# Keeping the emitted order of the matmuls in both feed-forward networks, from chunk 3 on

## The chip, the cores and the metric

The kernel runs on one core of one Trainium2 chip. A core has TensorE (PE in the profile, its weight loads PEld), VectorE (DVE), ScalarE (ACT), GpSimd (POOL), SyncE (SP, which here only issues transfers) and 16 DMA engines. The metric is the device time of one execution in microseconds (us); lower is better.

## The reference

One input x of 2048 tokens by 512 channels goes through two branches, and a gate for each token mixes their results:

```python
g = sigmoid((x * gate_w).sum(-1))
a = attention(x, wqkv) @ wo          # 32 heads of 16; each token looks at 8 keys, 2 tokens apart
b = (gelu(x @ w_gate) * (x @ w_up)) @ w_down      # 512 -> 1792 -> 512
out = g * a + (1 - g) * b
```

Everything is float32.

## The kernel before

The tokens are split into two parities of 1024 tokens (`par` 0 and 1). Since the attention's keys lie an even number of tokens apart, each parity is an attention problem of its own. The whole runs in one stream: the projections of parity 0, the feed-forward network (FFN) of parity 0 with `ffn(0)`, the projections of parity 1, `ffn(1)`, and the output projection. The attention of eight units (two parities by four groups of heads) is vector work on DVE; the generator `attention` hands it out piece by piece, and `pull` places pieces of it among the matmuls. The first DVE operation of a piece is `paced` (L357): it waits until the matmul that was emitted last before it has run.

Each FFN goes over 14 chunks `f` of 128 hidden channels. In a chunk, `gate_up` (L557) computes gate and up for two halves of 512 tokens by seven block products instead of eight; the operands a11, a12, a22 come from x itself (tiles A), and s1 to s4 are sums of blocks of x (tiles S); b11, b21, b22 and t1 to t4 are the weights and their sums (tiles g). Every operand is split into a high and a low part, so that `product` (L490) issues six matmuls: two blocks of 128 channels, and for each high by high, high by low and low by high. Each matmul streams 512 columns. The result of a product stands in a PSUM bank "p", of which there are four.

Around the products stand, in this order of emission: a11 (bank X, copied by ACT into bank W at L575), s1 (bank Z), the product a22 of the chunk before (`fourth`, L520, runs the closure `last` of L603), s2 (X), a12 (W, then gelu on ACT, L590), s4 (Z, then `add`, L505, on DVE), and s3 (X, then `add`). `hidden` (L508) makes the hidden values of a half: a multiplication on DVE (L509), the high part on ACT (L511, tile hh) and the low part on DVE (L512, tile hl). The first half is finished in its own chunk, after s4; the second half after a22, which is emitted in the next chunk.

The down projection takes the chunks by pairs `gr`. `down` (L527) handles 128 tokens: six matmuls, three for each chunk of the pair (hh by the high weights, hh by the low weights, hl by the high weights; tiles hh, hl and d), into one of the four banks "acc" for the first token half (b = 0), and into a bank "p" for the second (b = 1), where ACT copies the sum so far in (L532) and out again (L554). From chunk 2 on, each chunk emits four such pieces: chunk f handles the pair f // 2 - 1, so an even chunk f is the first to use the hidden values and weights of chunk f - 1. I call the four pieces of a chunk D0 and D1 (first half) and D2 and D3 (second half). The last pair follows after chunk 13, as eight pieces in a row.

The weights are prepared a chunk ahead: `fetch` and `fetch_d` load them (SP), `combine` (L430) forms the sums t1 to t4 on DVE, `operands` (L439) writes the negated low part on ACT and adds the raw weights with an accumulating DMA that POOL issues (L453, tiles g), and `down_w` (L478) does the same for the down weights (L481 on ACT, L482 on POOL, tiles d). L481 is paced behind s1.

What is emitted is not what runs in this order. The program is built with `schedule_with_timeline_sim=True`: a scheduler plays it through on a simulated timeline and lays down, for each engine, the order in which the instructions are ready there, with the emitted order as priority. `ordered` (L360) adds a dependency without a semaphore: it only tells the scheduler that an instruction stands behind another on the same engine. `LAST` holds the matmul that was emitted last.

```python
def ordered(ins, other):
    after(ins, other, mybir.DependencyClass.NoSync)
...
                if gr == 1 and b == t == 0 and not par:
                    ordered(ins, LAST[-1])
```

Before the change only the six matmuls of one piece (pair 1, first tile, parity 0) are ordered so.

Of the kernel before, what the change touches and what calls it, by code (L numbers as in the profile page):

```python
# [47 lines left out]
def tile_gated_mix(ctx: ExitStack, tc: tile.TileContext, xt, wqkv, wff, wo, out):  # L48
    nc = tc.nc
# [10 lines left out]
    def tl(tag, dt=F32):  # L60
        return pool.tile([P, COLS.get(tag, 512)], dt, name=tag, bufs=BUFS[tag])
# [5 lines left out]
    def bank(tag):  # L67
        return psum.tile([P, 512], F32, name=tag, bufs=BUFS.get(tag, 1))
# [5 lines left out]
    LAST = []  # L74
    idle = [bank("p") for _ in range(4)]
    for i in range(WARM):
        c = i // 4 % 2 * QW
        LAST[:] = [nc.tensor.matmul(idle[i % 4][:, c:c + QW], warm[:, :P], warm, start=not c, stop=True,
                                    skip_group_check=True)]
# [171 lines left out]
    def project_one(par, jj):  # L251

        ps = bank(f"acc{jj % BT}")
        qkv_mm(ps, par, jj, 2, range(KC))
        take(ps, par, jj, 1, False, tag=None if jj < 5 else "c")
        pull(2.2)
        if jj == NP - 1:
            done.add((par, 2))
# [93 lines left out]
    def after(ins, other, cls=mybir.DependencyClass.Sync):  # L352

        tc.add_manual_dep(ins.ins, other.ins.name, mybir.DependencyInfo(cls, mybir.DependencyReason.SCHED_ONLY),
                          reason="pace")
# [4 lines left out]
    def ordered(ins, other):  # L360
        after(ins, other, mybir.DependencyClass.NoSync)
# [39 lines left out]
    def pull(budget, key=None):  # L401
        credit[0] += budget
        while credit[0] > 0 and (key is None or key not in done):
            with tc.high_priority(offset=-BEHIND):
                c = next(fill, None)
            if c is None:
                credit[0] = 0.0
                return
            credit[0] -= c
        if key:  # L410
            credit[0] = 0.0
# [27 lines left out]
    def operands(par, f, i):  # L439


        n = len(GROUPS[i]) * QW
        w = tl(f"g{i}", F32R)
        hi, lo = w[:, :n], w[:, n:2 * n]
        for k, op in enumerate(GROUPS[i]):
            WG[f, op] = hi[:, k * QW:(k + 1) * QW], lo[:, k * QW:(k + 1) * QW]
        if par and not i:
            nc.sync.dma_start(w[:, :2 * n].bitcast(F32), WS[f, i])
            yield
            return  # L450
        raw = RAW[f][:, (0, 4)[i] * QW:][:, :n]
        nc.scalar.activation(lo, raw, AF.Copy, scale=-1.0)  # L452
        nc.gpsimd.dma_start(lo.bitcast(F32), raw, accum_op=OP.add)  # L453
        if not i:
            KEEP[f] = w[:, :2 * n]
        yield
        ins = nc.scalar.activation(hi, raw, AF.Copy)  # L457
        if f:
            paced(ins)
# [30 lines left out]
    def product(ps, a, w, start):  # L490
        for kc in range(2):
            ah, al = XOP[a, kc]
            wh, wl = (x[:, kc * P:(kc + 1) * P] for x in w)
            for n, (w_, a_) in enumerate(((wh, ah), (wh, al), (wl, ah))):
                LAST[:] = [nc.tensor.matmul(ps, w_, a_, start=(start and kc == 0 and n == 0),  # L495
                                            stop=(kc == 1 and n == 2), skip_group_check=True)]

    def copy(ps):
        s = tl("s")
# [12 lines left out]
        nc.vector.tensor_tensor(hl_, ge, hh_.bitcast(F32), op=OP.subtract)  # L512
        Hs[key] = hh_, hl_

    late, COPIED = [], []

    def pace(par, f):
        return PACE[2 if par else f > 5]

    def fourth():  # L520
        if late:
            late.pop()()
# [4 lines left out]
    def down(par, gr, t, b):  # L527
        if b == t == gr == 0:
            ACC.update((t, bank(f"acc{t}")) for t in range(BT))
        pp = bank("p") if b else ACC[t]  # L530
        if b and gr:
            nc.scalar.activation(pp, RT[BT + t], AF.Copy)  # L532
        ts = slice(t * P, (t + 1) * P)
        for i in range(2):
            hh_, hl_ = Hs[2 * gr + i, b]
            d = WD[2 * gr + i]
            for n, (a, w) in enumerate(((hh_, d[:, :512]), (hh_, d[:, 512:1024]), (hl_, d[:, :512]))):
                ins = nc.tensor.matmul(pp, a[:, ts], w, start=(i == 0 and n == 0 and gr == 0),  # L538
                                       stop=(i == 1 and n == 2), skip_group_check=True)
                if gr == 1 and b == t == 0 and not par:  # L540
                    ordered(ins, LAST[-1])
                LAST[:] = [ins]
        jj = BT * b + t
        if gr == NG - 1 and par:
            nc.scalar.activation(pp, pp, AF.Copy, scale=gc[:, par, jj:jj + 1])
            ACC[jj] = pp
        elif gr == NG - 1:
            st = tl("s")
            nc.scalar.activation(st, pp, AF.Copy, scale=gc[:, par, jj:jj + 1])
            nc.gpsimd.dma_start(out_v[2 * jj], st)  # L550
        elif b:
            if gr == 0:
                RT[BT + t] = tl("rt")
            nc.scalar.activation(RT[BT + t], pp, AF.Copy)  # L554
        pull(1.2 * pace(par, 2 * gr + 2))
# [87 lines left out]
    def ffn(par):  # L643
        XOP.update(((n, kc), X[par, blk, kc + k]) for n, blk, k in (("a11", 0, 0), ("a12", 0, 2), ("a22", 1, 2))
                   for kc in range(2))
        todo = iter(())
        for f in range(FC):
            do = {}

            def at(i, x, *args):  # L650
                do.setdefault(i, []).append(lambda: x(*args))

            if f > 1:
                pieces = [[lambda b=b, i=i: down(par, f // 2 - 1, f % 2 * 2 + i, b)] for b in range(2) for i in range(2)]
            else:
                tile_ = (lambda jj: project_one(1, jj)) if par else values
                pieces = [[lambda jj=jj: tile_(jj) for jj in jjs]
                          for jjs in (((0, 1), (2, 3), (4, 5), ()),
                                      ((6,), (7,), (), ()) if par else ((6, 7), (), (), ()))[f]]
            if f + 1 < FC:  # L660
                for i in range(2):
                    steps = operands(par, f + 1, i)
                    at(1 + 2 * i - (not par and f == 1), next, steps, None)
                    at(5 + i - (not par and f == 1), next, steps, None)
                at(0 if f != 1 else 5, fetch_d, f + 1)
                if f == 1 and not par:
                    for g_ in range(2):
                        at(3, down_split, g_)
                for g_ in ((), (0, 1) if par else ())[f] if f < 2 else (f,):
                    steps = down_w(g_)  # L670
                    at(2 if f > 2 else 4, next, steps, None)
                    at(7, next, steps, None)
            else:
                steps = down_w(f)
                at(1, next, steps, None)
                at(4, next, steps, None)
            if par:
                if f + 2 < FC:
                    at(0, fetch_sums, f + 2)
                else:  # L680
                    at(0, fetch_o) if f + 2 == FC else None
                if f + 1 == FC:
                    todo = chain(load_o(), channels_of(0, 0))
                    for i in range(1, 9):
                        at(i, next, todo, None)
            else:
                if f + 2 < FC:
                    at(1, fetch, f + 2)
                    at((4, 5, 6)[f] if f < 3 else 8, combine, f + 2)
                else:  # L690
                    at(0, fetch_x, 1, f + 2 - FC)
                if f + 1 < FC:
                    do.setdefault(0, []).insert(0, lambda: keep(f + 1))
                at(0, keep_parts, f)
                if f + 2 == FC:
                    at(8, early)
                if f + 1 == FC:
                    todo = before()
                    for i in range(2, 9):
                        at(i, next, todo, None)  # L700
            gate_up(par, f, pieces, do)
        for _ in todo:
            pass
        fourth()
        if par:
            out_first()
            oT = {}
        for b in range(2):
            for t in range(BT):
                down(par, NG - 1, t, b)  # L710
                if par and t == 0:
                    oT[0, b] = channels(par, 0, b)
                if not par and not b:
                    split_kq() if t % 2 else again(0, 1 + t)
                elif not par and b:
                    again(1, (2, 3, 0, 1)[t])
        if par:
            finish(oT)
# [452 lines left out]
```

## Time and profile before

| what | value |
|---|---|
| median of three runs | 608.14 us (606.92 to 609.78) |
| the profiled execution | 609.76 us |
| span of its profile, first to last instruction | 608.0 us |
| PE busy | 598.2 us, 2802 matmuls |
| DVE busy | 526.5 us |
| ACT busy | 382.9 us |
| POOL busy | 79.1 us |
| mean granted TensorE clock | 0.999 |

The profiled execution lasts 1.76 us longer than its span, and it stands near the upper end of the three runs. PE is the engine whose waits count. Its busy time is that of pipelined instructions: a matmul is shown with 0.39 us while the next begins after 0.23 us, so a wait shows as a gap in the starts rather than as idle time of the same length. In the rows below, L495 is a product, L538 a piece of the down projection, and the letters after the arrow are the operands.

### The profile page before, as it was taken

Reading aid. Unit: us, or ns where it says so; the run is one execution under the profiler, and the core shown is the slowest. Engines: PE = TensorE matmul, PEld = TensorE weight load, DVE = VectorE, ACT = ScalarE, POOL = GpSimd, SP = SyncE. Lnnn points to the kernel's source line nnn. Section 1 sums busy time; section 2 is a strip of 40 time slices with the busy share of each in tenths; the row PEclk is TensorE's granted clock in tenths of the full one; section 3 lists DMA queues with packets and bytes.
Section 4 is the critical chain, followed back from the end, with each engine's and each line's share of the span. In section 5 each row is a group of like instructions: output and inputs, shape, how many; then the busy total and the mean of one; then the engine's idle time right before and its main releaser. Section 6 shows DMA issues by size and latency. Waiting matters only on the chain.

```text
span 608.0 us, 8192 instructions
## 1 busy us (share of the span) xinstructions
PE 598.2 (98%) x2802; PEld 498.2 (82%) x2802; DVE 526.5 (87%) x611; ACT 382.9 (63%) x650; POOL 79.1 (13%) x106
## 2 busy tenths in 40 slices
PE   9999999999999999989999999999999999999997
PEld 6889977788888887877899888888888888888885
DVE  5997969999898998798989988789899999999941
ACT  5845557777679776857364356566866676677531
POOL 0501001111111111102000001111101111101200
PEclk9999999999999999999999999999999999999999
DMA  7289896989889888976789979686888768937823
GB/s 279 85 252 246 241 275 172 271 237 271 206 248 260 223 255 230 253 205 181 253 218 335 252 221 271 146 256 158 228 207 213 207 182 217 259 88 207 125 50 138
DMA packets 84741, 131.03 MB, mean 216 GB/s; under 512 B 8030, under 2 KB 52317, under 8 KB 84700
## 3 DMA queue, kind: packets, MB, share of 16 engines
q1 hardware_dynamic: 63310, 94.01, 47.7%
q0 software_dynamic: 12096, 31.40, 27.3%
q10 hardware_dynamic: 9294, 5.11, 2.8%
q8 instruction: 22, 0.36, 0.2%
q14 instruction: 19, 0.16, 0.1%
HBM read 67.18 MB, written 36.77 MB: 171 GB/s over the span
## 4 chain that ended last, share of the span: by engine, by line
PE 71%; DMA 12%; issue 8%; DVE 4%; ACT 3%; SPq 1%; ACTq 0%; POOL 0%; POOLq 0%; DVEq 0%
PE p L495 29%; PE p L538 9%; PE acc L189 9%; PE acc L538 9%; PE p L767 5%; DMA d<-r 4%; DMA g<-raw 3%; PE p L834 3%; PE acc L834 3%; DMA ws<-g 3%; DVE prod L290 2%; PE p L189 2%; PE acc L767 2%; DMA kq<-qs 1%; DMA vs<-hl 1%
## 5 line engine op out<-in xcount | busy, mean ns | idle before, releaser
L495 PE MATMUL p<-S,g 128*128 128x512 f32 x672 | 166.5, 390 | 0.0
L495 PEld LDWEIGHTS p<-S,g 128*128 128x128 f32 x672 | 125.7, 188 | 26.5 <-ACT rt L554 0.5
L495 PE MATMUL p<-A,g 128*128 128x512 f32 x504 | 127.6, 390 | 0.1
L495 PEld LDWEIGHTS p<-A,g 128*128 128x128 f32 x504 | 94.3, 188 | 20.4 <-DMA g<-raw 0.6
L290 DVE TENSOR_TENSOR prod<-kq 128x2048 f32<-128x2048 f32 x32 | 73.0, 2281 | 12.3 <-DMA kq<-qs 4.6
L453 POOL DMA_DIRECT2D g<-raw x40 | 34.8, 870 | 319.0 <-ACT g L452 180.5
L331 DVE TENSOR_TENSOR prod<-v,lg 128x2048 f32<-128x2048 f32 x32 | 72.9, 2277 | 1.8 <-PE acc L538 1.3
L293 DVE TENSOR_REDUCE lg<-prod 128x128 f32<-128x2048 f32 x32 | 73.0, 2282 | 0.3
L538 PE MATMUL p<-d,hh 128*128 128x512 f32 x224 | 68.0, 390 | 1.0 <-ACT p L532 0.5
L538 PE MATMUL acc<-d,hh 128*128 128x512 f32 x224 | 61.3, 392 | 3.3 <-DMA d<-r 2.9
L538 PEld LDWEIGHTS acc<-d,hh 128*128 128x128 f32 x224 | 41.8, 188 | 13.5 <-DMA d<-r 3.8
L538 PEld LDWEIGHTS p<-d,hh 128*128 128x128 f32 x224 | 41.9, 188 | 10.5 <-ACT p L532 0.9
L457 ACT ACTIVATE g<-raw 128x1024 fp32r<-128x1024 f32 (+1 forms) x40 | 39.5, 990 | 13.3 <-PE p L495 13.3
L509 DVE TENSOR_TENSOR c<-c 128x512 f32<-128x512 f32 x56 | 38.2, 683 | 9.2 <-ACT c L606 8.8
L505 DVE TENSOR_TENSOR c<-p,s 128x512 f32<-128x512 f32 x56 | 37.9, 682 | 8.1 <-PE p L495 8.1
L500 ACT ACTIVATE s<-p 128x512 f32<-128x512 f32 x56 | 33.2, 592 | 18.1 <-PE p L495 16.5
L452 ACT ACTIVATE g<-raw 128x1024 fp32r<-128x1024 f32 (+1 forms) x40 | 39.5, 986 | 7.9 <-DVE raw L434 6.9
L538 PE MATMUL p<-d,hl 128*128 128x512 f32 x112 | 42.3, 390 | 0.0
L512 DVE TENSOR_TENSOR hl<-c,hh 128x512 fp32r<-128x512 f32 x56 | 38.3, 685 | 4.5 <-ACT hh L511 4.2
L511 ACT ACTIVATE hh<-c 128x512 fp32r<-128x512 f32 x56 | 35.1, 626 | 7.4 <-DVE c L509 6.5
L554 ACT ACTIVATE rt<-p 128x512 f32<-128x512 f32 x48 | 28.1, 592 | 18.1 <-PE p L538 17.8
L335 DVE TENSOR_TENSOR prod<-prod 128x1024 f32<-128x1024 f32 x32 | 39.0, 1219 | 0.3
(193 smaller groups left out, 916.2 us busy)
## 6 DMA issues: line engine op xcount, KB each, us to landing
g<-raw POOLq DMA_DIRECT2D x27, 512.0 KB, 6.1
raw<-wff SPq DMA_DIRECT2D x42, 256.0 KB, 3.4
ws<-g SPq DMA_DIRECT2D x14, 768.0 KB, 5.6
g<-ws SPq DMA_DIRECT2D x14, 768.0 KB, 5.1
r<-wff SPq DMA_DIRECT2D x28, 256.0 KB, 3.7
d<-r POOLq DMA_DIRECT2D x26, 256.0 KB, 7.2
g<-raw POOLq DMA_DIRECT2D x13, 384.0 KB, 7.5
v<-vs SPq DMA_DIRECT2D x8, 512.0 KB, 7.3
```

The costliest lines, as they stand in the source:

```text
L189: LAST[:] = [nc.tensor.matmul(ps[:, :cn], a[:, t], w[:, c0:c0 + cn], start=(kc == 0 and n == 0), stop=(kc == KC - 1 and n == 2))]
L290: paced(nc.vector.tensor_tensor(prod, spans(k, jj), q[:, jj:jj + 2, None, :].to_broadcast([P, 2, W, UC]), op=OP.mult))
L293: nc.vector.tensor_reduce(two_of(lg, jj), prod.rearrange("p j w (h d) -> p (j w) h d", d=DH), axis=AX.X, op=OP.add)
L331: paced(nc.vector.tensor_tensor(prod.rearrange("p j w (h d) -> p (j w) h d", d=DH), spans(v, jj).rearrange("p j w (h d) -> p j w h d", d=D ...
L335: nc.vector.tensor_tensor(prod[:, :, :4], prod[:, :, :4], prod[:, :, 4:], op=OP.add)
L452: nc.scalar.activation(lo, raw, AF.Copy, scale=-1.0)
L457: ins = nc.scalar.activation(hi, raw, AF.Copy)
L495: LAST[:] = [nc.tensor.matmul(ps, w_, a_, start=(start and kc == 0 and n == 0), stop=(kc == 1 and n == 2), skip_group_check=True)]
L509: nc.vector.tensor_tensor(ge, ge, up, op=OP.mult)
L512: nc.vector.tensor_tensor(hl_, ge, hh_.bitcast(F32), op=OP.subtract)
L538: ins = nc.tensor.matmul(pp, a[:, ts], w, start=(i == 0 and n == 0 and gr == 0), stop=(i == 1 and n == 2), skip_group_check=True)
L767: ins = nc.tensor.matmul(pa, a, b, start=(first and n == 0), stop=(last and n == 2), skip_group_check=True)
```

## The change

From chunk 3 on in both FFNs, each matmul of a product and of a down piece is ordered behind the matmul emitted before it. In parity 0 this also covers all pieces of the pairs from 1 on, the eight closing ones among them; the eight closing pieces of parity 1 are not covered. No instruction is added or taken away, and no semaphore wait is asked for; the scheduler gets a fixed order for PE in these stretches, and orders the other engines against it anew.

```diff
@@ product
-                LAST[:] = [nc.tensor.matmul(ps, w_, a_, start=(start and kc == 0 and n == 0),
-                                            stop=(kc == 1 and n == 2), skip_group_check=True)]
+                ins = nc.tensor.matmul(ps, w_, a_, start=(start and kc == 0 and n == 0), stop=(kc == 1 and n == 2),
+                                       skip_group_check=True)
+                if KEPT:
+                    ordered(ins, LAST[-1])
+                LAST[:] = [ins]
...
-    late, COPIED = [], []
+    late, COPIED, KEPT = [], [], []
@@ down
-                if gr == 1 and b == t == 0 and not par:
+                if gr and not par or KEPT:
                     ordered(ins, LAST[-1])
                 LAST[:] = [ins]
@@ ffn
         for f in range(FC):
             do = {}
+            KEPT[:] = [f] if f > 2 else []
...
         fourth()
+        KEPT.clear()
         if par:
             out_first()
```

## The prediction, made before the result was known

> **What bounds the kernel now.** I read the page first, then PE's windows by chunk, PE's waits, and the timeline of single chunks.
>
> ```profile
> span 608.0 us, 8192 instructions
> ...
> PE 598.2 (98%) x2802; PEld 498.2 (82%) x2802; DVE 526.5 (87%) x611; ACT 382.9 (63%) x650; POOL 79.1 (13%) x106
> ...
> PEclk9999999999999999999999999999999999999999
> ```
>
> PE is busy 98% of the span, at full clock in every slice. How much room is left in the stretches that the change touches is told by the pace of the matmuls. The chain of waits has a run without a gap, and the windows give the chunks (us, PE busy and count; the last three columns are clock, DMA share, GB/s):
>
> ```profile
> 576.90 5.44 PE p L538 x24
> ```
>
> ```profile
> 104.18:150.33 46.15, 46.12 (x201) 1.00 0.95 255
> ...
> 165.29:180.68 15.39, 15.26 (x68) 1.00 0.87 240
> ...
> 210.60:225.56 14.96, 14.96 (x68) 1.00 0.86 247
> 225.56:242.09 16.53, 15.27 (x68) 1.00 0.98 246
> ...
> 257.05:284.32 27.27, 25.09 (x109) 1.00 0.66 195
> ```
>
> 24 matmuls in 5.44 us are 0.2267 us each: a group of six takes 1.36 us, a chunk of eleven groups (seven products, four down pieces) 14.96 us. The chunk at 210.60 takes just that and waits for nothing. The one at 165.29 loses 15.39 - 14.96 = 0.43 us, the one at 225.56 loses 1.57 us, and the close of the first FFN, 18 groups or 24.48 us, loses 2.79 us (the 109th record begins before the window). The sum, **4.8 us or 0.8%**, is all that an order can win in the first FFN; chunks 3 to 5, up to 150.33, are busy 46.12 of 46.15 us. In the second it can win nothing; PE is busy throughout (PE, PEld, DVE, ACT, POOL):
>
> ```profile
> 391.78:551.06 159.28, 159.28 (x704) 132.00 (x703) 147.89 (x154) 107.15 (x174) 18.36 (x22) 1.00 0.76 204
> ```
>
> [...]
>
> Who caused the 4.8 us is in PE's waits (total, times, longest) and in the timeline:
>
> ```profile
> PE acc L538 <- DMA d<-r: 2.9, 2, 1.7
> PE p L538 <- ACT p L532: 0.5, 1, 0.5
> ...
> PEld acc L538 <- DMA d<-r: 3.8, 2, 2.1
> ...
> PEld p L495 <- DMA g<-raw: 0.6, 1, 0.6
> ```
>
> ```profile
> 210.60 2.88 PE L495 MATMUL p<-A,g 128*128 128x512 f32 x12
> 213.32 1.97 PE L538 MATMUL acc<-d,hh 128*128 128x512 f32 x8
> ...
> 216.04 2.88 PE L495 MATMUL p<-S,g 128*128 128x512 f32 x12
> ...
> 221.48 2.88 PE L495 MATMUL p<-S,g 128*128 128x512 f32 x12
> ...
> 225.56 2.88 PE L495 MATMUL p<-A,g 128*128 128x512 f32 x12
> 228.28 0.39 PE L538 MATMUL acc<-d,hh 128*128 128x512 f32 x1
> 229.93 1.89 PE L538 MATMUL acc<-d,hh 128*128 128x512 f32 x7 [1.26 <-DMA d<-r]
> ...
> 260.49 1.89 PE L538 MATMUL acc<-d,hh 128*128 128x512 f32 x7 [1.68 <-DMA d<-r]
> ...
> 275.35 0.73 PE L538 MATMUL p<-d,hh 128*128 128x512 f32 x2 [0.50 <-ACT p L532]
> ```
>
> The reader is to see an order that is not the emitted one. A chunk runs a11 and the old a22 (A, x12), then twelve matmuls on "acc", then s1 and s2, a12, D2, s4 and s3, D3. Eight high-part matmuls in a row on "acc" cannot be D0 and D1 as emitted, whose low parts stand between. Counting groups back from 284.32 us, where the FFN ends, the "acc" work at 228.28 (chunk 11) and 258.41 (chunk 13) is the half of the next pair that needs only the even chunk just finished. So the scheduler pulls it a chunk ahead, onto down weights whose accumulating transfer has not landed.
>
> **The change part by part.** It adds no instruction, DMA or semaphore; nothing moves past the queues of SP or POOL except by what the scheduler orders anew. The order becomes a11, D0, s1, old a22, s2, D1, a12, s4, D2, s3, D3.
>
> *What goes.* The pulled-ahead use goes: an even chunk's weights are first used two chunks later. I count the chunk's 1.57 and the row's 1.68 us. The wait for ACT's copy into a bank "p" (0.50) sits in the closing pieces; four pieces on "acc" now stand ahead of those on "p" and cover it. Together 3.75, **3.8 us**. The 0.43 us at 165.29 stay: a11's third matmul waits for the weights' transfer, and a11 keeps its place.
>
> *Odd chunks' down weights* are still used one chunk on. Their rows in chunk 10, their transfers in the chain, and the median on the page:
>
> ```profile
> 218.09 0.62 ACT L481 ACTIVATE d<-r 128x512 fp32r<-128x512 f32 x1
> ```
>
> ```profile
> 219.00 10.88 DMA d<-r
> ...
> 249.64 10.80 DMA d<-r
> ```
>
> ```profile
> d<-r POOLq DMA_DIRECT2D x26, 256.0 KB, 7.2
> ```
>
> L481 is paced behind s1, which now ends 4.08 us into the chunk and not 6.80. At best the issue moves from 8.40 (219.00 - 210.60) to 5.7 us, and the slow 10.88 us land at 16.6. D0 of the next chunk needs them in its fifth matmul, at 14.96 + 1.36 + 0.91 = 17.2: in time. If POOL keeps its order (L482 behind two transfers of L453), landing is at 8.4 + 10.9 = 19.3, 2.1 us late; with the median, 15.6, in time. So from 0 to two slow transfers at 2.1 = 4.2 us; I take 0, by the median row.
>
> *The hidden values are what is late next.* For an even chunk the emitted order gives each half one distance. First half: from the end of s4 come D2, s3, D3, a11 and five matmuls until D0 reads hl: 4 x 1.36 + 1.13 = **6.57 us**. Second half: from the end of a22 come s2, D1, a12, s4 and five matmuls to D2's hl, again 6.57. Between lie add or gelu, multiplication, hh and hl, with attention pieces of about 2.3 us queued on DVE in between. Four readings, first half in chunk 11 of the second FFN and chunk 10 of the first, second half of chunks 7 and 9:
>
> ```profile
> 517.36 0.62 PE L538 MATMUL p<-d,hh 128*128 128x512 f32 x2
> ...
> 518.77 0.68 DVE L505 TENSOR_TENSOR c<-p,s 128x512 f32<-128x512 f32 x1
> 519.37 2.27 DVE L293 TENSOR_REDUCE lg<-prod 128x128 f32<-128x2048 f32 x1
> ...
> 521.56 0.68 DVE L505 TENSOR_TENSOR c<-p,s 128x512 f32<-128x512 f32 x1
> ...
> 524.96 0.68 DVE L512 TENSOR_TENSOR hl<-c,hh 128x512 fp32r<-128x512 f32 x1
> ```
>
> ```profile
> 226.97 0.69 DVE L512 TENSOR_TENSOR hl<-c,hh 128x512 fp32r<-128x512 f32 x1
> ```
>
> ```profile
> 183.40 1.52 PE L495 MATMUL p<-S,g 128*128 128x512 f32 x6
> ...
> 184.78 1.28 ACT L606 ACT_TABLE_LOAD   x1
> ...
> 190.97 0.68 DVE L512 TENSOR_TENSOR hl<-c,hh 128x512 fp32r<-128x512 f32 x1
> ```
>
> ```profile
> 216.44 0.68 DVE L512 TENSOR_TENSOR hl<-c,hh 128x512 fp32r<-128x512 f32 x1
> ```
>
> s4 ended at 517.36 and hl at 525.64: 8.28 us, **1.71 late** by the new distance. In chunk 10 s4 ended at 222.84 (half of the x12 at 221.48) and hl at 227.66: 4.82, in time. a22 ended at 183.40 and hl at 191.65, a table load between: 8.25, 1.68 late. a22 ended at 213.32 and hl at 217.12: 3.80. Before, PE ran other groups meanwhile; now it must stand still.
>
> Such first uses are 22: five even chunks (4 to 12) and the ordered close in the first FFN, five in the second, two halves each. The ends are 0 and half of them at 1.7, 18.7 us. In the new order D2 stands between s4 and s3, so the multiplication need not queue behind the second add (0.68); that leaves about 1.0 us of the 1.7. I choose one in five late by 1.0: 22 / 5 x 1.0 = **4.4 us**.
>
> *Sum:* 609.76 - 3.8 + 4.4 = 610.4 for the profiled execution; on the median, 608.14 + 0.6 = **608.7 us**.
>
> *After the FFNs* PE's time decides up to the end, where the last attention values are split and used:
>
> ```profile
> 588.94 0.69 DVE L87 TENSOR_TENSOR hl<-raw,hh 128x512 fp32r<-128x512 f32 x1 [2.71 <-ACT hh L86]
> ...
> 593.06 0.62 PE L767 MATMUL acc<-S,hh 128*128 128x512 f32 x2
> ```
>
> Between 589.63 and 593.06 lie 3.4 us. A win beyond that would meet DVE there, unless the paced attention moved up with PE, which its 10% of idle time allows.
>
> **The rivals.** *All operands in time:* readings like 4.82 and 3.80 are the rule; only the 3.8 us act: 604.3, with the whole 4.8 us 603.3. For it: the emitted order spaces the evacuations evenly. Against: DVE is 93% busy in the second FFN (147.89 of 159.28). *The hidden values come late as a rule:* the first half's chain through DVE, read by D0, is late by the 1.0 us above in all eleven first uses: 11.0 - 3.8 = +7.2, 615.3. It decides once the 22 uses lose more than 3.8 + 3.0 = 6.8 us, 0.31 each. For it: the 8.28 and 8.25 above, and that the second FFN, where nothing can be won, has five of the eleven. [...] *The scheduler had this order anyway:* against it stands the timeline above; 608.1.
>
> **How the numbers follow.** A measurement of this kernel tells about 0.5%, 3.0 us, from no change. The forecast, wins and new waits within 3 us of each other, has 0.42; the same order anyway 0.03; all in time 0.27; late as a rule 0.26; the clock 0.02. So faster 0.27, same 0.45, slower 0.28. Cases of both signs hold over half, so the likeliest one's own range is 605.1 to 611.2. The wide range goes from 603.5, near the whole win, to 615.0, just under the late case: it leaves out a small part of the first rival, half of the late one, and the clock.
>
> **What would show it.** Right: the timeline of a chunk shows eleven groups of six in the emitted order; no PE wait for d in chunks 11 and 13; PE waits for L512 or L511 ("hl", "hh") ahead of L538 in even chunks, each under 2 us, some four or five; in the second FFN chunks longer than 14.96 us where there were none. Wrong: no waits for hidden values (then 604), or waits in odd chunks or at s1 and a22 for a bank "p", which I hold for covered since D3's copy out of its bank has the 2.7 us of a11 and D0; or DVE, pushed back, ending the kernel.

## The result and the profile after

| | before | after |
|---|---|---|
| median | 607.97 us (606.92 to 609.78, 4 runs) | 624.87 us (623.0 to 628.63, 4 runs) |
| profiled execution / span | 609.76 / 608.0 us | 625.36 / 623.5 us |
| mean granted clock | 0.999 | 0.991 |

The ratio is 1.028, interval 1.0242 to 1.0317: **slower by 2.8%**. The time lies outside the range on record. Lines below the first edit have moved down by a few: the down matmuls are L541 now, add L508, multiplication L512, hh L514, hl L515.

The page of after, span, busy times and clock by slice:

```profile
span 623.5 us, 8180 instructions
...
PE 604.3 (97%) x2802; PEld 499.6 (80%) x2802; DVE 527.0 (85%) x611; ACT 384.4 (62%) x650; POOL 79.2 (13%) x106
...
PEclk9999998999999999999999999999998999999999
```

The work is the same (the counts of instructions on PE, DVE, ACT and POOL have not moved). PE's busy time grew by 6.1 us though it runs the same 2802 matmuls, and two slices of the clock show an 8: some matmuls ran slower (0.427 us each at 107.99 us, in the last section, in place of 0.2267). PE's waits say what it stood still for (total, times, longest):

```profile
PE acc L541 <- DVE hl L515: 5.3, 6, 1.4
PE p L541 <- DVE hl L515: 2.5, 2, 1.8
PE p L495 <- DVE c L508: 2.0, 2, 1.4
PE p L541 <- ACT hh L514: 1.5, 1, 1.5
PE acc L541 <- ACT hh L514: 1.3, 2, 1.0
```

The waits for the down weights (2.9) and for the copy into a bank "p" (0.5) are gone, and in their place stand 10.6 us for hh and hl and 2.0 us for adds. The timeline of PE in one chunk of the second FFN, where nothing was late:

```profile
437.83 1.52 PE L495 MATMUL p<-A,g 128*128 128x512 f32 x6
439.19 0.61 PE L541 MATMUL acc<-d,hh 128*128 128x512 f32 x2
439.64 0.39 PE L541 MATMUL acc<-d,hl 128*128 128x512 f32 x1
...
440.55 1.52 PE L495 MATMUL p<-S,g 128*128 128x512 f32 x6
```

a11, D0 with its low parts between, s1: the emitted order, group by group, each 1.36 us after the other. Where nothing is late, the order costs nothing; what costs is an operand that is late for it.

**A list of gaps** does the accounts. A gap is the start of a row of matmuls, less the start of the row before and its matmuls at 0.2267 us (0.1203 for 256 columns; e4 has 24 of 256 or 258 columns in 2.89 us from 308.90 us on); gaps over 0.12 us count. A stretch at half clock counts as a gap too, since its matmuls take longer than that (0.427 us each in after at 107.99 us). The gaps were summed from the PE timeline of each profiled execution, in us ("all" has those before 80 us as well):

| kernel | 80 to 112 us | 112 to 300 | 300 to 575 | all | span |
|---|---|---|---|---|---|
| before | 2.0 | 4.6 | 0 | 10.1 | 608.0 |
| before, second profile | 1.2 | 1.8 | 0 | 6.7 | 604.6 |
| after | 8.5 | 4.6 | 8.1 | 24.7 | 623.5 |
| e1 first FFN only | 8.6 | 6.1 | 0 | 17.9 | 616.3 |
| e2 second FFN only | 1.6 | 2.2 | 7.8 | 14.8 | 613.2 |
| e3 products only | 5.1 | 4.5 | 1.2 | 14.2 | 612.8 |
| e4 down pieces only | 5.1 | 3.1 | 2.0 | 13.3 | 611.5 |
| e5 D0 later | 7.1 | 1.3 | 1.6 | 13.5 | 611.4 |
| e6 D0 later, from chunk 4 | 2.4 | 3.0 | 1.6 | 10.2 | 607.9 |
| e7 the same, first FFN only | 3.6 | 2.9 | 0 | 9.6 | 607.5 |
| e8 the same, from chunk 10 | 1.8 | 3.5 | 0 | 8.4 | 606.3 |
| e9 the change from chunk 4 | 2.9 | 10.1 | 6.7 | 23.1 | 621.5 |
| e10 beginnings only | 2.2 | 4.3 | 0.5 | 10.6 | 608.7 |
| e12 hh on DVE | 8.8 | 15.8 | 13.6 | 41.6 | 640.8 |
| e13 after, scores cut | 1.0 | 2.5 | 0.8 | 7.8 | 605.6 |
| e14 before, scores cut | 0.9 | 9.1 | 1.3 | 14.4 | 612.0 |
| e15 hl on POOL | 9.7 | 6.4 | 10.2 | 29.6 | 628.6 |
| e16 after, halves | 0 | 8.3 | 2.4 | 13.9 | 612.2 |
| e17 e6, halves | 0.1 | 9.0 | 4.3 | 16.7 | 614.8 |
| e18 before, halves | 0 | 6.5 | 6.4 | 16.2 | 615.8 |

Span less gaps is 597.6 to 599.6 us in all twenty: to within 2 us, every kernel here is one amount of matmul time plus the gaps of PE, and the gaps after 575 us are nothing in each. 14.6 of the 15.5 us between the two spans are in the list, so it can be read by place.

**The start at chunk 3, +6.5 us.** The same stretch of PE, first before, then after:

```profile
103.15 1.19 PE L538 MATMUL p<-d,hh 128*128 128x512 f32 x4 [0.47 <-ACT hh L511]
104.18 3.05 PE L495 MATMUL p<-A,g 128*128 128x512 f32 x12
107.07 0.61 PE L538 MATMUL p<-d,hl 128*128 128x512 f32 x2
```

```profile
103.45 1.69 PE L541 MATMUL p<-d,hh 128*128 128x512 f32 x4 [1.54 <-ACT hh L514]
106.97 1.22 PE L541 MATMUL p<-d,hl 128*128 128x512 f32 x2 [1.82 <-DVE hl L515]
107.99 2.76 PE L495 MATMUL p<-A,g 128*128 128x512 f32 x6
```

The hl of the last pieces of chunk 2 is used at 107.07 in the one and at 106.97 in the other. DVE finished it at 106.3 before and at 106.9 after, so it is late in both. Before, PE filled the time with twelve product matmuls that were emitted later; now they may not pass. This row is DVE's in before:

```profile
105.64 0.68 DVE L512 TENSOR_TENSOR hl<-c,hh 128x512 fp32r<-128x512 f32 x1
```

DVE of after shows why it is late:

```profile
101.14 0.64 DVE L512 TENSOR_TENSOR c<-c 128x512 f32<-128x512 f32 x1
...
102.62 2.28 DVE L293 TENSOR_REDUCE lg<-prod 128x128 f32<-128x2048 f32 x1
...
105.02 0.69 DVE L508 TENSOR_TENSOR c<-p,s 128x512 f32<-128x512 f32 x1
105.62 0.68 DVE L512 TENSOR_TENSOR c<-c 128x512 f32<-128x512 f32 x1
106.22 0.69 DVE L515 TENSOR_TENSOR hl<-c,hh 128x512 fp32r<-128x512 f32 x1
```

The multiplication at 101.14 is that of the awaited half. Between it and its low part at 106.22 stand a reduction of the attention, 2.28 us, and an add and a multiplication for another half (105.02 and 105.62).

**D0 of even chunks, 8.1 us in six places**, 2.2 in the first FFN (1.46 us in chunk 4, 0.71 in chunk 8) and 5.9 in the second (chunks 4, 8, 10, 12). The rows of DVE, ACT and PE that make up the chain in chunk 8 of the second:

```profile
469.55 0.68 DVE L512 TENSOR_TENSOR c<-c 128x512 f32<-128x512 f32 x1
...
470.15 2.28 DVE L293 TENSOR_REDUCE lg<-prod 128x128 f32<-128x2048 f32 x1
...
470.27 0.63 ACT L514 ACTIVATE hh<-c 128x512 fp32r<-128x512 f32 x1 [0.38 <-DVE c L512]
...
470.95 0.73 PE L541 MATMUL acc<-d,hh 128*128 128x512 f32 x2 [1.00 <-ACT hh L514]
...
472.35 0.68 DVE L515 TENSOR_TENSOR hl<-c,hh 128x512 fp32r<-128x512 f32 x1
...
473.09 0.80 PE L541 MATMUL acc<-d,hl 128*128 128x512 f32 x1 [1.40 <-DVE hl L515]
```

While ACT makes hh from c (0.63 us), DVE has nothing of this chain to do and begins a reduction of 2.28 us; hl comes after it. PE waits 1.00 and 1.40 us in one piece.

That is one place of six, and the six are not alike. DVE in chunk 4 of the second FFN, where the first add is at 403.30:

```profile
403.90 2.29 DVE L290 TENSOR_TENSOR prod<-kq 128x2048 f32<-128x2048 f32 x1
406.10 0.68 DVE L512 TENSOR_TENSOR c<-c 128x512 f32<-128x512 f32 x1
406.70 0.68 DVE L508 TENSOR_TENSOR c<-p,s 128x512 f32<-128x512 f32 x1
407.30 2.28 DVE L293 TENSOR_REDUCE lg<-prod 128x128 f32<-128x2048 f32 x1
409.49 0.68 DVE L515 TENSOR_TENSOR hl<-c,hh 128x512 fp32r<-128x512 f32 x1
```

In all four places of the second FFN an attention operation of 2.3 us stands between the first add and the multiplication, and another between the multiplication and hl: 2.3 us in chunks 4, 8 and 12, 1.2 us in chunk 10. In the two places of the first FFN three short operations stand between the multiplication and hl, 1.8 us in chunk 4 and 2.0 us in chunk 8, and no long one. In all six the second add (that of s3) runs ahead of hl, before the multiplication or after it. So hl is late by the sum of what the scheduler put ahead of it on DVE, and not by one reduction alone.

**The rest:** 1.55 us ahead of a22 of chunk 13 for the add that reads its bank X, 0.78 at the second FFN's start, 0.77 at two products a11 in the first FFN that wait for their weights' transfer; and the clock, below. Against them stand the 4.6 us of before that went.

### The profile page after: what moved, and what is told of

Same layout as the page of the kernel before. It is cut to its first block, busy times and chain, and to the rows that moved or that the text cites. A ratio compares the mean times of both kernels' runs of the same rounds, so it can differ in the third digit from the quotient of the medians.

```text
span 623.5 us, 8180 instructions
## 1 busy us (share of the span) xinstructions
PE 604.3 (97%) x2802; PEld 499.6 (80%) x2802; DVE 527.0 (85%) x611; ACT 384.4 (62%) x650; POOL 79.2 (13%) x106
## 4 chain that ended last, share of the span: by engine, by line
PE 64%; DVE 16%; DMA 8%; issue 6%; ACT 4%; SPq 1%; ACTq 0%; DVEq 0%; POOL 0%; POOLq 0%
PE p L495 28%; PE acc L189 9%; PE acc L541 9%; PE p L541 8%; PE p L772 5%; DVE prod L290 4%; DMA g<-raw 3%; DVE lg L293 3%; DMA raw<-wff 2%; PE acc L772 2%; PE p L189 2%; DVE c L512 1%; DVE hl L515 1%; DVE c L508 1%; DMA kq<-qs 1%
## 5 line engine op out<-in xcount | busy, mean ns | idle before, releaser
L495 PE MATMUL p<-S,g 128*128 128x512 f32 x672 | 171.5, 392 | 0.9 <-DVE c L508 0.6
L495 PE MATMUL p<-A,g 128*128 128x512 f32 x504 | 130.8, 393 | 1.6 <-DVE c L508 1.4
L541 PE MATMUL p<-d,hh 128*128 128x512 f32 x224 | 69.4, 393 | 1.9 <-ACT hh L514 1.5
L541 PE MATMUL acc<-d,hh 128*128 128x512 f32 x224 | 69.1, 391 | 1.3 <-ACT hh L514 1.3
L541 PEld LDWEIGHTS p<-d,hh 128*128 128x128 f32 x224 | 42.0, 188 | 11.7 <-ACT hh L514 2.0
L541 PEld LDWEIGHTS acc<-d,hh 128*128 128x128 f32 x224 | 42.1, 189 | 11.2 <-ACT hh L514 2.1
L512 DVE TENSOR_TENSOR c<-c 128x512 f32<-128x512 f32 x56 | 38.3, 684 | 13.9 <-ACT c L609 13.4
L541 PE MATMUL acc<-d,hl 128*128 128x512 f32 x112 | 44.1, 398 | 5.3 <-DVE hl L515 5.3
L482 POOL DMA_DIRECT2D d<-r x26 | 22.4, 871 | 210.6 <-ACT d L481 119.6
L541 PE MATMUL p<-d,hl 128*128 128x512 f32 x112 | 44.0, 396 | 2.5 <-DVE hl L515 2.5
L515 DVE TENSOR_TENSOR hl<-c,hh 128x512 fp32r<-128x512 f32 x56 | 38.3, 684 | 5.4 <-ACT hh L514 5.1
L514 ACT ACTIVATE hh<-c 128x512 fp32r<-128x512 f32 x56 | 35.1, 627 | 8.6 <-DVE c L512 8.1
L508 DVE TENSOR_TENSOR c<-p,s 128x512 f32<-128x512 f32 x56 | 37.9, 683 | 2.4 <-PE p L495 2.4
```

The source lines that it names most:

```text
L495: ins = nc.tensor.matmul(ps, w_, a_, start=(start and kc == 0 and n == 0), stop=(kc == 1 and n == 2), skip_group_check=True)
L508: nc.vector.tensor_tensor(c, ps, s, op=OP.add)
L512: nc.vector.tensor_tensor(ge, ge, up, op=OP.mult)
```

## The experiments

My theory (A) was: what the order costs is a wait for hidden values that are made too late on DVE, at D0 of even chunks and at the start. The rivals: the transfers or the clock, other costs of any order, and the halves of the change acting on each other. Every ratio is to the kernel before, timed beside it on the same chip.

**e1, e2: one FFN each.**

```diff
-            KEPT[:] = [f] if f > 2 else []
+            KEPT[:] = [f] if f > 2 and not par else []      # e1; e2: "and par"
```

e2 also takes the old condition of one piece for parity 0 again.

> The order is kept in the first FFN only. Theory A (each stretch pays for its own waits: operands of the next matmul are not there yet, and PE may not take another one): the gaps between PE's matmuls between 90 and 300 us sum to 11.6 us in the changed kernel and 6.1 in the one before, so about 608 + 5.5 + 1 = 614 to 615 us, with the clock drop at 104 us and none later. Rival B (the new order of the other engines sets DVE back over the whole run, and the second FFN pays for what the first one did): 620 or more, or gaps in the second FFN although its order is free. Rival C (only one place costs, the start at chunk 3): as A here, but the other half alone would then cost little.

> The order is kept in the second FFN only; the first is as before. Theory A: the gaps of the second FFN in the changed kernel, 7.7 us against none, so 608 + 7.7 = 615 to 616 us, waits for hl ahead of the sixth matmul of D0 in even chunks. Rival B: over 620 or under 611. Rival C: 609 to 611.

e1 616.59 us, ratio 1.0161 (1.0143 to 1.0179); e2 616.37, 1.015 (1.0117 to 1.0183). The two add up to 3.1%, which the intervals do not part from the 2.8%, and each has about the gaps that after has in that FFN (in e1, two transfers cost 1.8 us where they cost 0.8 in after). e2 keeps its clock at 1.00, so most of the loss is waits.

**e4, e3: down pieces or products alone.** In e4 the two new lines in `product` are taken out; in e3 the condition in `down` is the old one.

> Only the down pieces are ordered behind the matmul emitted before them; products may be taken early while a down piece waits. Theory A: PE has products to run while hidden values are late, so the waits at D0 go; and the pulled-ahead use of an even chunk's down weights stays forbidden, so the 1.4 and 1.9 us waits of chunks 11 and 13 stay away: 604 to 609 us. Rival B (fixing any part upsets the schedule of the other engines): 615 or more.

> The products ordered among themselves and behind the last down piece emitted, the down pieces' own matmuls free but for the one piece of before. Theory A (the dear part is a down piece that must run at its emitted place with its youngest hidden value): D0 may slip behind the next product only as far as that product is not ordered behind it; since each product is ordered behind the down piece's last matmul, the waits stay nearly whole: 618 to 624. Theory E (the down pieces' inner order makes the waits): without it 608 to 612.

e4 613.63, 1.0106 (1.0083 to 1.013); e3 613.88, 1.0108 (1.0089 to 1.0126). Theory A missed both. In e4 D0 no longer waits for hidden values, since products may slip ahead of it, but products wait for banks "p" instead: 1.7 us twice for ACT's copy out (L555). In e3 the PE timeline shows how the wait is filled:

```profile
216.28 1.98 PE L541 MATMUL acc<-d,hh 128*128 128x512 f32 x8
218.09 0.39 PE L541 MATMUL acc<-d,hl 128*128 128x512 f32 x1
```

Other high parts are drawn together ahead of the one young hl. Either half of the freedom saves 10 to 11 us of the 17; neither alone saves all.

**e5: D0 later.** All stays ordered, but D0 is emitted after s2, beside D1.

```diff
         idle(1, 0.7)
-        piece(0)
+        if not KEPT:
+            piece(0)
...
         idle(3, 0.7)
+        if KEPT:
+            piece(0)
         piece(1)
```

> Everything stays in emitted order, but from chunk 3 on D0 is emitted after s2, next to D1: four groups more between a chunk's s4 and the first use of its hidden values, 10.7 us in place of 6.6. Theory A: the waits at D0 of the even chunks go (1.5 at 127 us, 0.7 at 188, 1.4 at 409, 2.9 and the clock's share 1.7 at 470, 0.7 at 504, 1.0 at 535: 9.9 us); the start at chunk 3 (5.5) and a22 of chunk 13 (1.6) stay: 625 - 9.9 = 615 us. Rival B (the chain through DVE is simply behind, and waits move to the next reader): 620 or more, with waits at a22, D1 or D2 instead.

613.51, 1.0109 (1.0092 to 1.0126). D0 now comes three groups (s1, a22 and s2, 4.1 us) later, and its waits in even chunks are gone (112 to 300 us 4.6 to 1.3; 300 to 575 us 8.1 to 1.6). The start stays, 7.1 us.

**e6 to e9: where the order begins.** e6 is e5 with the first FFN ordered from chunk 4; e7 leaves the second FFN free besides; e8 is e7 from chunk 10; e9 is the change itself from chunk 4.

```diff
-            KEPT[:] = [f] if f > 2 else []
+            KEPT[:] = [f] if f > 2 + (not par) else []      # e6, e9
+            KEPT[:] = [f] if f > 3 and not par else []      # e7; e8: f > 9
```

e8 also limits the condition in `down` to pairs above 3 and the old piece.

> D0 after s2 as in e5, and in the first FFN the order starts at chunk 4 instead of chunk 3. Theory A (the start in e5 and after is dear because it falls on the boundary between an even and an odd chunk: chunk 2's D2 and D3 must be finished before chunk 3's first product, and they read hidden values of chunk 1 that were made a few us ago): at chunk 4 the pieces that stand before the boundary are those of chunk 3, whose hidden values are over a chunk old, so the waits at 98 to 111 us go (5 us of 7.1) and no like wait comes at the boundary of chunk 4: 613.5 - 5.0 = 608.5, clock 1.000. Theory B (an order costs wherever it begins, since the free order has run ahead): the same 5 us turn up a chunk later, 613.5.

> As e6, but the second FFN is left free, with the old order of emission. Theory A: only the win of the change is left, the waits for d in chunks 11 and 13 (3.3 us) less what remains of waits in 112 to 300 us in e5 (1.1): 607.0 - 3.3 = 603.7, with up to 1 us back: 603.7 to 605. Second FFN as before, no wait. Theory B (start costs anywhere): 609.

> D0 after s2 and the order only from chunk 10 of the first FFN on. Theory A: the same waits for d go, the boundary before chunk 10 has chunk 9's pieces with old hidden values: 603.7 to 605, like e7. Theory B (a start costs 5 us anywhere): 609, with waits of 1 us or more between 210 and 220 us.

> The change itself (D0 where it was) with one size changed: the first FFN is ordered from chunk 4 on. Theory A: the start's 6.5 us (8.5 against 2.0 between 80 and 112 us, part of it at half clock) goes, the waits at D0 of even chunks stay in both FFNs: 624.9 - 6.5 = 618.4. Theory B: the start's waits move to the boundary of chunk 4: 624 to 625.

| run | us | ratio (interval) |
|---|---|---|
| e6 | 610.16 | 1.0044 (1.003 to 1.0058) |
| e7 | 609.22 | 1.0023 (1.0014 to 1.0033) |
| e8 | 608.48 | 1.0014 (1.0 to 1.0029) |
| e9 | 623.67 | 1.0266 (1.0239 to 1.0293) |

e9 refutes the part of theory A that laid the start on the boundary of chunks 2 and 3: begun at chunk 4, the same loss turns up at that chunk's D0 (gaps of 2.67 for hh, 1.54 with a transfer, then 2.07 at a slower pace: the six matmuls at 125.86 us take 2.56 us, 0.427 each). With D0 later (e6) the start shrinks to 1.83 us, for a bank "p". So at both places where the order was begun with D0 left where it was, a hidden value was late; what differs is which matmul read it first. In e8, begun at chunk 10 with D0 later, none was waited for in the ordered stretch. e7 and e8 have fewer gaps than the before that I had profiled (9.6 and 8.4 against 10.1) and yet are no faster than the medians of before. That pointed at the reference.

**Before once more, and a least change (e10).** e10 is before with only the first matmul of each first-half piece of pairs 5 and 6 ordered:

```diff
-                if gr == 1 and b == t == 0 and not par:
+                if not par and (gr == 1 and b == t == 0 or gr > 4 and not b and i == n == 0):
```

> The kernel before once more, for a second profile. The profiled execution shown before the prediction took 609.76 us, 2 us over the typical 607.4. Theory C (its waits for the down weights in chunks 11 and 13, 1.42 and 1.85 us, are a matter of that execution's transfers): in an execution near 607 us these waits are shorter by about 2 us together, and what the change could take away on the median was 2 us and not 3.8. Theory D (they are in every execution): both waits again at 1.3 to 1.9 us, and the 2 us lie elsewhere.

> The kernel before, with the first matmul of each first-half down piece of pairs 5 and 6 in the first FFN ordered behind the matmul emitted before it; all else free. It takes away only the early use of the down weights in chunks 11 and 13. Theory D: no wait for d there, 607.4 - 3.3 = 604.1, and nothing late in its place since the scheduler may still put other groups between. Theory C: 607.4 - 1 to 2 = 605.5 to 606.5. Either way it would be a version faster than both. A rival (each order written in costs elsewhere): 608 or more.

The second profile of before took 606.33 us. Its waits for d:

```profile
PE acc L538 <- DMA d<-r: 0.9, 1, 0.9
```

One wait of 0.9 us where the first profile had two, 2.9 us together. Theory C holds in kind: these waits differ from execution to execution, and in this one the change could take away 1.7 us (gaps of 1.02 and 0.66), not 3.8. But this execution is itself 1.4 us under the median of the runs beside it (607.7), so on the median the room lies somewhere between the two. e10 took 611.34, 1.0064 (1.0037 to 1.009): the wait for d in chunks 11 and 13 is gone, but a product waits for its weights' transfer instead:

```profile
PE p L495 <- DMA g<-raw: 2.7, 1, 2.7
```

The rival was right: a few written edges have the scheduler lay out the other engines anew, and the next late transfer shows. In both profiles of before the order of the instructions on each engine is the same; in e10 it is the same up to 228 us and then differs on PE, DVE, ACT and POOL. POOL there issues a transfer of down weights ahead of those of the product's weights, and the second of these goes out at 249.77 us, where before it went out at 248.12.

**e12, e15: the chain on other engines.** In odd chunks from 3 on, hh of the first half is made by DVE (e12), or hl by POOL (e15).

```diff
-        nc.scalar.activation(hh_, ge, AF.Copy)
+        if KEPT and key[0] % 2 and not key[1]:          # e12
+            nc.vector.tensor_copy(hh_, ge)
+        else:
+            nc.scalar.activation(hh_, ge, AF.Copy)
...
-        nc.vector.tensor_tensor(hl_, ge, hh_.bitcast(F32), op=OP.subtract)
+        eng = nc.gpsimd if KEPT and key[0] % 2 and not key[1] else nc.vector      # e15
+        eng.tensor_tensor(hl_, ge, hh_.bitcast(F32), op=OP.subtract)
```

> The change itself, but from chunk 3 on in odd chunks the high part hh of the first half is made by DVE and not by ACT, right behind the multiplication; eleven operations of some 0.68 us are added to DVE and as many taken from ACT. Theory A2 (D0's hl is late because DVE puts a reduction of the attention, 2.28 us, between the multiplication and hl while hl waits for ACT's hh): c, hh and hl run back to back, hl is ready 1.5 to 2 us sooner, the waits at D0 of even chunks (8.1 us in the list of gaps) shrink to 2 or less and the second drop of the clock goes: 624.9 - 6 to 8 = 617 to 619. Theory A3 (the multiplication itself comes too late, behind an attention product): waits shrink by under 3 us, 622 to 625.

> The change with the low part hl of the first half made by POOL in odd chunks from 3 on, instead of by DVE: the chain is then multiplication on DVE, hh on ACT, hl on POOL, and no attention operation of DVE can stand between hh and hl. Theory A2: the waits for hl at D0 (acc, 5.3 us in the list of waits) go, those for hh at D0 (1.3) stay: 624.9 - 5 to 7 = 618 to 620, if POOL needs under 1.5 us for one. Theory A3 (multiplication too late by itself): 623 to 626. If POOL needs 2 us or more, the waits move there and nothing is won.

e12 took 641.71, 1.0567 (1.0546 to 1.0588): both theories missed, on the far side. DVE and PE of e12, chunk 8 of the second FFN:

```profile
482.91 0.69 DVE L512 TENSOR_TENSOR c<-c 128x512 f32<-128x512 f32 x1
...
483.51 2.28 DVE L293 TENSOR_REDUCE lg<-prod 128x128 f32<-128x2048 f32 x1
485.71 0.42 DVE L515 CAST hh<-c 128x512 fp32r<-128x512 f32 x1
...
486.27 0.70 PE L544 MATMUL acc<-d,hh 128*128 128x512 f32 x2 [2.96 <-DVE hh L515]
```

The cast takes 0.42 us, but the scheduler put the reduction between c and the cast, so now hh too waits behind it, and one place costs 2.96 us. The run moved the chain into the reduction's way, not out of it. e15 took 629.37, 1.0324 (1.0272 to 1.0375). POOL's group of e15 and PE's wait for it:

```profile
L516 POOL TENSOR_TENSOR hl<-c,hh 128x512 fp32r<-128x512 f32 x12 | 18.0, 1503 | 94.5 <-ACT hh L514 64.8 <-issue 15.2 <-PE p L495 8.1
```

```profile
PE acc L542 <- POOL hl L516: 7.4, 7, 2.5
```

POOL needs 1.50 us for what DVE does in 0.68, just at the limit that the expectation had named, and seven of its twelve results were waited for. It doesn't tell the theories apart.

**e13, e14: the score work cut.** Product and reduction of the attention's scores take 4 of the 16 keys of two rows; the other scores are zero. This leaves out three quarters of the attention's score work.

```diff
-            prod = pool.tile([P, 2, W, UC], F32, name="prod")
-            paced(nc.vector.tensor_tensor(prod, spans(k, jj), q[:, jj:jj + 2, None, :].to_broadcast([P, 2, W, UC]),
+            prod = pool.tile([P, 2, W, UC], F32, name="prod")[:, :1, :4]
+            paced(nc.vector.tensor_tensor(prod, k[:, None, jj:jj + 4], q[:, jj:jj + 1, None, :].to_broadcast([P, 1, 4, UC]),
...
```

> The change with the attention's score work on DVE cut to a quarter: product and reduction of the scores take 4 of each 16 keys of two rows (128x512 instead of 128x2048 elements, some 0.6 us instead of 2.28 each), the other scores are zero; all else, and the place of every piece, is kept. Theory A2 (the hidden values are late at D0 and at a22 because a 2.28 us attention operation stands between add, multiplication and hl on DVE): the waits at D0 in even chunks (8.1 us) and the a22 wait (1.55) go but for those behind the mixing products, which stay at 2.28: 3 us or less left; time 613 to 617. Theory A3 (the chain from s4 to hl is too long by itself for 6.57 us): waits as in the change, 622 to 625. The start at chunk 3 (6.5 us with the clock) is open: if attention pieces cause it too, it goes as well and the time is 607 to 610.

> The kernel before with the same cut of the score work, as the control for the run above: TensorE is full through both networks, so less DVE work gains little: 604 to 607.

e13, the change with the cut, took 606.3 us, 0.9962 (0.9936 to 0.9987): **all 17 us are gone**, at the start too, and the clock is 1.000. PE's longest waits of e13 inside the FFNs:

```profile
...
PE p L496 <- DVE c L509: 1.1, 1, 1.1
PE acc L542 <- DMA d<-r: 0.6, 1, 0.6
PE p L496 <- DMA g<-raw: 0.6, 1, 0.6
```

Not one wait for hh or hl is left among PE's waits. The chain from s4 to hl fits the distance when short operations stand around it, and is not too long by itself (A3). Whether their length did it (A2) or the lower load of DVE (431.8 us busy in place of 527.0) this run cannot tell. The control was a poor one: e14 took 614.17, 1.0077 (1.004 to 1.0114), because its scheduler put a split of down weights (L485) on ACT ahead of the copy of s1, and it waited there for its transfer; PE stood for 5.5 us.

**e16 to e18: the same work in halves.** Scores row by row, operations of 1.2 us instead of 2.28 (after, e6 and before).

```diff
-        for jj in range(0, NP, 2):
-            prod = pool.tile([P, 2, W, UC], F32, name="prod")
+        for jj in range(NP):
+            prod = pool.tile([P, 2, W, UC], F32, name="prod")[:, :1]
...
```

> The change with product and reduction of the scores done for one row instead of two at a time: twice as many operations of 128x1024 elements, some 1.2 us each, the same work on DVE (a little more for the extra starts). Theory A2, by the length of the one operation that stands in the way: each late hidden value is some 1.1 us less late, so the waits at D0 in even chunks fall from 8.1 to 2 or 3 us, the start at chunk 3 shrinks likewise and the clock stays at 1.00: 612 to 617. Theory A4, by the load of DVE as a whole (the cut run also took some 100 us of work off it): waits as in the change, 623 to 626.

> The same halves in the version with D0 after s2 and the first FFN ordered from chunk 4 (610.2): by A2 the waits that were left there (1.8 at the start, 0.9 at an a22, 0.8 at a22 of chunk 13, 0.8 and 0.6 in the second FFN) halve: 607 to 609; by A4 610 to 611.

> The control: the kernel before with the halves. TensorE has almost no waits there that these operations cause: 606 to 609 by both theories.

e16 615.5, 1.0135 (1.0104 to 1.0166); e17 616.3, 1.0149 (1.012 to 1.0179); e18 616.3, 1.0144 (1.0106 to 1.0181). Groups and waits of e16:

```profile
L290 DVE TENSOR_TENSOR prod<-kq 128x1024 f32<-128x1024 f32 x64 | 77.9, 1217 | 5.0 <-PE acc L189 1.7 <-PE acc L541 1.4 <-PE p L541 0.3
```

```profile
PE p L541 <- DVE hl L515: 3.1, 2, 1.9
PE acc L541 <- DVE hl L515: 2.1, 1, 2.1
```

DVE has 4.8 us more to do in this group alone, and still the gaps from 395 to 570 us, where after lost 7.3, are 0.13 us: D0 of the second FFN waits for nothing. There the length of the operations in the way counts (A2), and DVE's load (A4) does not explain the loss. In the first FFN it is otherwise. D0 of chunk 4 loses more than in after, 2.9 us in its two gaps against 1.5, and with them 1.6 us at a slower pace, since the twelve product matmuls from 120.83 us on take 4.34 us, 0.36 each:

```profile
120.49 0.50 PE L541 MATMUL acc<-d,hl 128*128 128x512 f32 x1 [2.13 <-DVE hl L515]
```

Four operations stand there between the multiplication (116.24) and hl (119.77), an add, a reduction of 1.20 us and two of 0.67 us, and the last two begin after ACT has finished hh. So short operations can make hl as late as a long one. The other numbers missed: the halves cost the kernel before 1.4% by themselves (e18; 2.8 us at a transfer of down weights and small ones), and e17 gained nothing, having met weights' transfers four times (2.9 us) and an add (3.0). With halves in both, e16 against e18, the order costs nothing that can be seen: 615.5 and 616.3. Their gaps lie in other places, though, so this is no proof that it is free.

No run beat the kernel before with the whole work done. With 1.7 to 3.8 us to be won and other transfers a microsecond behind, I see no version here that would.

## Why the prediction was wrong, point by point

- **Bound and room.** PE bounds the kernel, and nothing behind the FFNs took a loss or gain away: right in all twenty profiles. But the 4.8 us of room were those of one execution, some 2 us over the median. The second profile of before has 3.4 us less of gaps, and 2.2 of them are in the two waits for down weights. The prediction noted that it stood at the upper end and did not draw the conclusion.
- **What goes, 3.8 us.** Right in kind and, for that execution, in size: neither wait is in after. In the second profile of before it would have been 1.7.
- **Odd chunks' down weights, 0.** Right: no wait for d in after.
- **The step that failed first: the waits were counted only within the ordered stretch, and its beginning was put at nothing.** There PE had been filling a late hl with twelve later matmuls; held to the order it stood still. This place lost 6.5 us, the largest part of the miss.
- **The second step that failed: new waits, "one in five late by 1.0", 4.4 us.** Of the 22 first uses six were late, all first halves, by 8.1 us in the list, 1.35 each. The share, about one in four, was near; the lateness was too small. The discount from 1.7 to 1.0 rested on the multiplication not queueing behind the second add, and in all six places the second add ran ahead of hl after all. In the second FFN two attention operations came into the chain besides, one ahead of the multiplication and one in the time in which ACT makes hh. The prediction had named these pieces "of about 2.3 us queued on DVE in between" and did not ask where in the chain they could stand.
- **What else the sum left out.** The clock at 473 us (1.5), a22 of chunk 13 (1.55), the second start (0.78), two products a11 (0.77). The wait at a22 is one for its bank "p", which the prediction held for covered and had named as a sign of being wrong.
- **The rivals.** "Late as a rule" had the right reader (D0, first half) for half of the loss, but its 11 first uses at 1.0 less 3.8 gave 615.3; six were late. The chance of 0.02 for the clock had nothing of before behind it (0.999 over the run), and no run shows what brings a fall; in after the clock fell to half in two places, beside waits of 1.54 us (to 103.45 us) and of 1.00 and 1.40 us (to 470.95 and 473.09 us).
- **Sum as it came out:** 609.76 - 4.6 + 6.5 (start, with some 2.6 of clock) + 8.1 (D0) + 1.5 (clock at 473) + 1.55 + 0.78 + 0.77 + 0.14 (a small gap at 280 us) = 624.5; the profiled execution took 625.36, and 0.9 us are outside the list.

What stays open: why the free order of before has its lead in exactly these places, that is, how far the scheduler's own timeline agreed with the chip's; and whether part of e13's gain comes from the lower load besides the length, since its control was disturbed and e16 kept waits of 5.2 us for hl. No run put hl ahead of the attention work in DVE's order and left all else as it was, which would test the cause directly; each edit had the scheduler lay out all engines anew.

## What to carry to other kernels

Here the fixed order on the engine that bounds the kernel turned late operands into stops (1.54 and 1.82 us at the start of after), where the free order had filled the time (with twelve product matmuls); so before fixing it, list for each first use who makes the operand, and what else can stand on that engine ahead of it or begin in a hole of the chain (here 2.28 us in the 0.63 us in which another engine worked). Count the place where the order begins as well as those within it. And take the room to be won from two profiles or more, not from one execution.

## What the runs showed of the hardware

The granted clock fell to half in two places of after, beside waits of under 2 us. The first fall shows from 103.75 to 104.00 us (0.87, and 0.50 behind it), after a wait of 1.54 us that ended at 103.45 us; the second from 472.50 to 473.00 us (0.57), within the wait of 1.40 us that ended at 473.09 us, with one of 1.00 us shortly before. Windows of after (us, PE busy and count, clock, DMA share, GB/s):

```profile
104.00:106.00 2.00, 1.14 (x3) 0.50 1.03 193
...
472.00:474.00 2.00, 0.91 (x2) 0.64 0.87 305
474.00:476.00 2.00, 2.00 (x6) 0.50 0.01 3
```

At half clock the six matmuls at 107.99 took 2.56 us until the next row (110.55), 0.427 us each instead of 0.2267; the gaps that have no wait, or are longer than theirs, sum to some 2.6 us at the start (2.61 - 1.82 + 0.57 + 1.20) and 1.5 at 473 (0.37 + 1.09). What decides whether the clock falls was not shown, and the length of the waits alone does not tell it: the same two waits, 1.00 and 1.40 us, came with a clock of 0.50 in after and of 1.00 in e2 (461 to 470 us) and e9 (470 to 478 us). The fall at 104 us had PE busy up to 101.9 and again from 103.45 us, while one wait of 2.7 us in e10 left the clock alone (the windows around it):

```profile
250.00:252.00 2.00, 1.45 (x7) 1.00 1.06 250
252.00:254.00 2.00, 0.00 (x0) 1.00 1.05 384
254.00:256.00 2.00, 1.83 (x8) 1.00 1.08 245
```
